# Two slots' shift of a fused projection, with an older head, in an attention and feed-forward kernel

## The chip, the cores and the metric

The kernel runs on one core of a Trainium2 chip. The metric is the time of one execution on the device in microseconds (us). Three executions of the kernel before took 512.79, 513.41 and 513.46 us; the median is 513.41. A core has a matrix engine (PE, with its weight loads shown as PEld), a vector engine (DVE), an activation engine (ACT), a general engine (POOL) and an engine that only issues transfers (SP). They run their own instruction streams in program order and wait for each other through semaphores. The kernel fixes the order of each stream by hand.

## The reference

Attention over 8 batches and 8 heads of 576 rows and 64 columns, with a threshold, and then a feed-forward layer on the joined heads:

```python
scores = scale * np.matmul(q, k.transpose(0, 1, 3, 2))
thresh = np.max(scores, axis=-1, keepdims=True) - tau
scores = np.where(scores >= thresh, scores, -1000000000.0)
attn = np.exp(scores - max) ; attn = attn / (sum(attn) + 1e-09)
x = matmul(attn, v)             # 4608 tokens x 512, heads joined
h = x @ w_in                    # 512 x 2048
g = h * np.clip(h + 3.0, 0.0, 6.0) / 6.0
out = g @ w_out                 # 2048 x 512
```

All inputs and the output are float32.

## The kernel before

**Slots.** Two heads make a pair, two pairs a quad; there are 16 quads. A quad is worked in 9 slots: slots 0 to 3 are the four row tiles of 128 rows of its first pair, 4 to 7 those of the second, and slot 8 the remaining 64 rows of both. So there are 144 slots, numbered n = 0 to 143 in the loop from L539 on, and each holds 128 rows of two heads.

**One slot of attention.** `scores` (L283) multiplies Q by K on PE into PSUM: 576 columns for each of the two heads a, in two parts. `sm_max` (L302) copies a head's scores to SBUF on DVE and takes their row maximum (L310). `sm_bias` (L316) makes the threshold from the maximum on POOL (L317). `sm_mask` (L320) is a rectifier with a huge slope on ACT that rejects what is under the threshold (L322), `sm_exp` (L325) the exponential with its row sum on ACT (L327). `sm_recip` (L329) is a reciprocal on DVE (L330), `sm_norm` (L332) the normalisation to bfloat16 on POOL (L335). The result has to be transposed: by a DMA transpose that SP issues (L343), or, for slots marked `on_chip`, by nine transposes on PE (`pe_transpose`, L346) and a copy on DVE (L351). `av_main` and `av_rest` (L364, L372) multiply the transposed weights by V on PE (L359, L362), and DVE copies the product out as xT or xR (L370, L380). `products` (L507) lists in which slot each product stands.

**Score columns.** Up to slot N1 + 2 each head has one set of PSUM columns for its scores (128 onward for a = 1, 1664 onward for a = 0), so the scores of a slot wait for the maximum of the slot before. Later, odd slots use a second set, 704 and 2240 (`first`, `score_col`, L275 to L281). Slots 1 and 2 have columns of their own (L279), in which the head a = 0 does not wait for that of the slot before, and for these two slots `scores` finishes one head before it begins the other.

**The feed-forward layer.** A first projection item (`mm1`, L385) is 8 matmuls (L394) for two of the sixteen hidden blocks and 256 tokens, or 4 larger ones (L389) for the remaining rows of two batches. Its rectifier (`mm1_relu`, L399) is on ACT in even slots (L402) and on DVE in odd ones (L404); the gate (`mm1_gate`) is on DVE (L417). A finished group of items adds pieces of the second projection (`mm2_part`, L424) to a list: a piece is 4 matmuls (L428), and four pieces make a tile of the output, which is scaled, copied (L434, L436) and written by a DMA. Items are taken one a slot from slot N1 = 22 on (L586), pieces two in each even slot (`second`, L528). Items are put on the list by the products of a quad of odd number (L522 to L525). What the loop leaves over is worked off behind it (L694 to L710).

**Regimes.** From N1 on the order on ACT and DVE changes. Before, in slot n, ACT does the exponentials of slot n - 1 and then the masks of n; from N1 on the exponentials of n and then the masks of n + 1. In even slots from N1 to N2 = 28 DVE takes the maxima of two slots at once (L559, L573), and ACT's exponentials stand ahead of its rectifier (L578).

**Banks.** PSUM has 8 banks of 512 columns. HB = 6 takes the projection items, the PE transposes of on-chip slots and the warm-ups; OB = 7 accumulates the output, and takes the odd slots' items where no pieces were made in the slot before (L590). `bank()` (L216) hands out banks 2 and 5 in turn for transposes of Q and K and for products.

**Head.** `load_quad` (L83) loads Q and K of a quad by DMAs: `load_k`, `load_q`, `rest`. For quad 0 the first K and the rest of K are issued by ACT, everything else by SP. PE starts on two multiplications of a zero constant (L188 to L190) and 14 transposes of the identity (`warm_up`, L191), then it transposes K (L236), the first Q rows (L470), the rest of K (L471) and the other Q rows (L473). Weights of the layer are cast and loaded by DMAs that POOL issues (L165, L169), one or two a slot (L653 to L656).

Of the kernel before, what the change touches and what calls it, by code (L numbers as in the profile page):

```python
# [20 lines left out]
def kernel(  # L21
# [10 lines left out]
    nc = tc.nc  # L32
# [7 lines left out]
    NSLOT = 9  # L40
    NB = 2
    N0 = 3
    N1 = 22
    N2 = 28
    HB, OB = 6, 7
    scale = 1.0 / math.sqrt(D)
    tau = float(tau)
# [35 lines left out]
    def load_quad(quad):  # L83
        b, g = divmod(quad, 2)
        nat[quad] = (nat_pool.tile([P, 1152], F32, tag="nq", name="nq"),
                     nat_pool.tile([P, 4, 4, D], F32, tag="km", name="km"),
                     nat_pool.tile([P, 2 * D], F32, tag="kr", name="kr"))
        nq, km, kr = nat[quad]

        def main(dst, src, h, order, by=nc.sync):  # L90
            by.dma_start(out=dst[:, :, h, :], in_=src[b, 4 * g + h, 0:512, :].rearrange(order, t=4))

        def blocks_q(n, a, j):
            c = 32 * (2 * a + j)
            nc.sync.dma_start(out=nq[c:c + 32, n * S:(n + 1) * S].rearrange("p (k d) -> p k d", d=32),
                              in_=q[b, 4 * g + 2 * n + a, :, 32 * j:32 * j + 32].rearrange("(k r) d -> r k d", r=32))

        def blocks_k(n, a, j):
            c = 32 * (2 * a + j)
            nc.sync.dma_start(  # L100
                out=km[c:c + 32].rearrange("p t h d -> p (t h d)")[:, n * 512:(n + 1) * 512].rearrange(
                    "p (t m d) -> p t m d", t=4, d=32),
                in_=k[b, 4 * g + 2 * n + a, 0:512, 32 * j:32 * j + 32].rearrange("(m r t) d -> r t m d", r=32, t=4))

        def load_k(n):
            if b < NB:
                for a in range(2):
                    main(km, k, 2 * n + a, "(p t) d -> p t d", by=nc.scalar if quad == n == 0 else nc.sync)
            else:
                for a in range(2):  # L110
                    for j in range(2):
                        blocks_k(n, a, j)

        def load_q(n):
            if b < NB:
                for a in range(2):
                    main(nq[:, 0:1024].rearrange("p (t h d) -> p t h d", h=4, t=4), q, 2 * n + a, "(t p) d -> p t d")
            else:
                for a in range(2):
                    for j in range(2):  # L120
                        blocks_q(n, a, j)

        def rest():
            for dst, src in ((kr[:], k), (nq[:, 1024:1152], q))[0:2 if b < NB else 1]:
                for n in range(2):
                    by = nc.scalar if quad == 0 and src is k else nc.sync if quad < 5 else nc.gpsimd
                    by.dma_start(out=dst[64 * n:64 * n + 64, :].rearrange("p (h d) -> p h d", h=2),
                                 in_=src[b, 4 * g + 2 * n:4 * g + 2 * n + 2, 512:S, :].rearrange("h p d -> p h d"))
# [56 lines left out]
        for _ in range(count):  # L185
            nc.tensor.transpose(ps[:, HB, 0:P], identf[:], identf[:])

    blank = nc.const_aps.tensor(0.0, [P, P], F32)  # L188
    for _ in range(2):
        nc.tensor.matmul(ps[:, HB, 0:P], blank, blank, start=True, stop=True)  # L190
    warm_up(14)  # L191
    identb = singles.tile([P, P], BF16)
    nc.vector.tensor_copy(out=identb[:], in_=identf[:])
    three = singles.tile([P, 1], F32)
# [25 lines left out]


    def copy_out(out, in_):
        if 0 <= now < N1 + 2:
            nc.vector.tensor_copy(out=out, in_=in_)
        else:
            nc.scalar.copy(out=out, in_=in_)
# [49 lines left out]
        return n > N1 + 2 and n % 2 == 1  # L276

    def score_col(n, a):
        if n in (1, 2):  # L279
            return 1664 if a else 3200 if n == 1 else 128  # L280
        return (704 if first(n) else 128) + (0 if a else 1536)  # L281

    def scores(n):  # L283
        quad, slot = divmod(n, NSLOT)
        w0 = 320 if first(n) else 384
        parts = ((0, w0), (w0, S - w0))
        heads = range(2)
        for group in [((a,), parts) for a in heads] if n in (1, 2) else [(heads, (part,)) for part in parts]:
            for i in range(2 if slot == 8 else 1):
                for a, (k0, w) in [(a, part) for part in group[1] for a in group[0]]:  # L290
                    pair = 2 * quad + (i if slot == 8 else slot // 4)
                    rows = slice(64 * i, 64 * i + 64) if slot == 8 else slice(0, P)
                    q0 = 512 if slot == 8 else slot % 4 * P
                    c0, kc = score_col(n, a) + k0, 64 * (1 - a) + k0
                    nc.tensor.matmul(ps_flat[rows, c0:c0 + w],  # L295
                                     qT_of(pair)[a * 64:(a + 1) * 64, q0:q0 + rows.stop - rows.start],
                                     kT_of(pair)[a * 64:(a + 1) * 64, kc:kc + w], start=True, stop=True)
# [4 lines left out]
    def sm_max(sl):  # L302
        sl.s = s_pool.tile([P, 2, S], F32, tag="s", name="s")
        sl.m = stat_pool.tile([P, 2], F32, tag="m", name="m")
        sl.bias = stat_pool.tile([P, 2], F32, tag="bias", name="bias")
        sl.rsum = stat_pool.tile([P, 2], F32, tag="rsum", name="rsum")
        sl.rinv = stat_pool.tile([P, 2], F32, tag="rinv", name="rinv")
        for i in range(2):
            c0 = score_col(sl.n, i)
            nc.vector.tensor_scalar(out=sl.s[:, i, :], in0=ps_flat[:, c0:c0 + S],  # L310
                                    scalar1=1.0, scalar2=None, op0=Alu.mult, op1=Alu.max,
                                    accum_out=sl.m[:, i:i + 1])
            if sl.n < N0:
                sm_bias(sl, slice(i, i + 1))

    def sm_bias(sl, of=slice(0, 2)):  # L316
        nc.gpsimd.tensor_scalar(out=sl.bias[:, of], in0=sl.m[:, of], scalar1=-scale, scalar2=tau, op0=Alu.mult,  # L317
                                op1=Alu.add)

    def sm_mask(sl, i):  # L320
        s = sl.s[:, i, :]
# [142 lines left out]

    alloc_qk(0)
    evict = transpose_k(0)
    lead = ps[:, HB:HB + 2, :]
    q_main = nat[0][0][:, 0:1024].rearrange("p (t h d) -> p t h d", h=4, t=4)
    q_rows = bank()
# [14 lines left out]
    for quad in range(NQUAD):  # L484
        for slot in range(NSLOT):
            sl = Slot()
            sl.quad, sl.slot, sl.n = quad, slot, len(queue)
            sl.on_chip = len(queue) < N1 - 1 and (slot in (1, 3, 5, 7, 8) or slot == 0 and quad > 0)
            queue.append(sl)
    scores(0)  # L490
    sm_max(queue[0])
    scores(1)

    turns = {1: [("q", 1), ("k", 1)], 3: [("rest", 0)]}
# [13 lines left out]
    for quad in range(NQUAD):  # L508
        p0, p1 = 2 * quad, 2 * quad + 1
        if quad < NB:  # L510
            jobs = ((8, p0, 0, 512), (13 - 2 * quad, p1, 0, 512), (15 - 3 * quad, None, 0, 0))
        else:
            jobs = [(7 - quad % 2 + 2 * i, *of) for i, of in enumerate(
                ((p0, 0, 256), (p0, 256, 256), (p1, 0, 256), (p1, 256, 256), (None, 0, 0)))]
        for after, *of in jobs:
            products.setdefault(quad * NSLOT + after, []).append((quad, *of))
# [10 lines left out]

    def second():  # L528
        nonlocal pieces, bb, mt, part
        pieces = 2 if now % 2 == 0 and todo2 else 0  # L530
        for _ in range(pieces):
            bb, mt, part = todo2.pop(0)
            mm2_part(bb, mt, part)
# [5 lines left out]
    for n, sl in enumerate(queue):  # L539
# [18 lines left out]
        if n + 1 < len(queue):  # L558
            if n <= N1 or n > N2 + 1 or n % 2 == 0:  # L559
                sm_max(queue[n + 1])  # L560
            if n + 1 >= N0:
                sm_bias(queue[n + 1])
        even = n >= N1 and n % 2 == 0
        if n >= N0:
            sm_recip(prev)
# [20 lines left out]
        if todo1 and n >= N1:  # L586
            item, then = todo1.pop(0)
            if n == len(queue) - 2:
                second()
            h = mm1(item, 0 if n == len(queue) - 1 else OB if n > N1 and n % 2 and not pieces else HB)  # L590
            todo2.extend(then)
        else:
            item = None
# [42 lines left out]
            evict = []  # L636
        for out_of_psum in evict:
            out_of_psum()
        if n < N0:
            scores(n + 2)  # L640
            warm_up(6)
# [11 lines left out]
        if n < 4 or 15 < n < 20 or n > 33:  # L653
            start(vcasts, 1 if n < N1 or n % 2 else 0)
        else:
            start(casts, 2 if n in (5, 8, 11, 14) or 21 < n < 28 else 1)  # L656
        prev = sl

    last = NQUAD - 1
# [85 lines left out]
```

## Time and profile before

| | us |
|---|---|
| three executions | 512.79, 513.41, 513.46 |
| median | 513.41 |
| the profiled execution | 512.79 |
| its span, first to last instruction | 511.0 |
| busy: PE, DVE, ACT, POOL | 503.4, 442.8, 450.3, 298.6 |
| one maximum on DVE (L310), mean | 0.748 |
| one mask, one exponential on ACT (L322, L327), mean | 0.762, 0.671 |
| one normalisation on POOL (L335), mean | 0.743 |
| one gate on DVE (L417), one rectifier on ACT (L402), mean | 0.687, 0.686 |
| one matmul of an item (L394), of a piece (L428), mean | 0.273, 0.379 |

Durations in the groups run from an instruction's start to its end. Neighbours on an engine overlap at their edges, so the distance from one start to the next is shorter: 0.60 for a gate of 0.69, and for a row of 8 item matmuls 0.98 in all. The chain of waits gives such distances. A line of the chain or the timeline has the start in us, the duration or stretch, the engine, the line of the kernel and how many instructions are taken together; in brackets stand the idle time before it and what ended it. In the stretches the number in front of (x..) is an engine's busy time.

### The profile page before, as it was taken

To read this page: it belongs to the slowest core of one execution; us is meant where nothing else is said; L and a number is where in the kernel's file an instruction comes from. 1 tells how busy PE (TensorE), PEld (TensorE's weight loads), DVE (VectorE), ACT (ScalarE), POOL (GpSimd) and SP (SyncE) were. 2 spreads that over 40 slices of the span, in tenths; PEclk is the share of its full clock that TensorE was granted. 3 is DMA by queue.
4 is the path that set the end of the run, shared out by engine and by line. 5 is a ranking of instruction groups with operands and counts; after the bars stand their busy time and mean duration, and the time that the engine had idled before them with its cause. 6 is when DMAs were issued, how large, how long until landed. Compare 5 with 4: busy or idle time off the path is not lost.

```text
span 511.0 us, 12107 instructions
## 1 busy us (share of the span) xinstructions
PE 503.4 (99%) x4132; PEld 319.8 (63%) x4132; DVE 442.8 (87%) x1127; ACT 450.3 (88%) x977; POOL 298.6 (58%) x539
## 2 busy tenths in 40 slices
PE   8999999999999999999999999999999999999997
PEld 7656566666655666666655666666655666667564
DVE  4788899989999999999999999999999999887251
ACT  4999999999999999999999999999999999987160
POOL 2788879666666756656565656666566755552000
PEclk9999999999999999999999999999999999999999
DMA  6998999989999999999899999999999996563132
GB/s 144 182 172 147 153 143 182 174 157 178 188 160 172 163 174 160 205 162 181 150 158 181 154 163 163 179 169 175 163 178 149 187 177 116 114 111 75 72 57 77
DMA packets 314318, 78.77 MB, mean 154 GB/s; under 512 B 296880, under 2 KB 309424, under 8 KB 314256
## 3 DMA queue, kind: packets, MB, share of 16 engines
q1 hardware_dynamic: 294464, 67.90, 78.0%
q0 software_dynamic: 18304, 9.64, 15.6%
q8 instruction: 32, 0.52, 0.4%
q10 hardware_dynamic: 1488, 0.46, 0.4%
q14 instruction: 30, 0.25, 0.2%
HBM read 36.70 MB, written 9.44 MB: 90 GB/s over the span
## 4 chain that ended last, share of the span: by engine, by line
PE 80%; DVE 4%; ACT 3%; issue 1%; DVEq 0%
PE ps L295 24%; PE ps L428 23%; PE ps L394 20%; PE ps L359 7%; PE ps L389 3%; DVE s L310 1%; PE ps L362 1%; ACT s L327 1%; ACT s L322 1%; DVE g L417 1%; DVE r L404 1%; PE ps L668 1%; ACT r L402 1%; PE ps L350 0%; DVE xT L370 0%
## 5 line engine op out<-in xcount | busy, mean ns | idle before, releaser
L335 POOL TENSOR_SCALAR pn<-s,rinv 128x576 bf16<-128x576 f32 x288 | 210.6, 743 | 19.4 <-issue 4.8
L310 DVE TENSOR_SCALAR_CACHE_REDUCE s<-ps 128x576 f32<-128x576 f32 x288 | 205.0, 748 | 13.4 <-POOL pn L335 5.1
L322 ACT ACTIVATE s<-s,bias 128x576 f32<-128x576 f32 x288 | 205.7, 762 | 3.6 <-POOL bias L317 3.2
L327 ACT ACTIVATE s<-s 128x576 f32<-128x576 f32 x288 | 192.5, 671 | 0.3
L295 PE MATMUL ps<-kT,qT 64*128 64x384 f32 (+7 forms) x1280 | 175.5, 419 | 2.1 <-DVE s L310 2.0
L295 PEld LDWEIGHTS ps<-kT,qT 64*128 64x128 f32 (+1 forms) x1280 | 103.7, 175 | 57.8 <-issue 15.6
L394 PE MATMUL ps<-xT,w_in_sb 128*128 128x256 bf16 x1024 | 131.0, 273 | 0.6 <-DVE g L417 0.5
L428 PE MATMUL ps<-w_out_sb,g 128*128 128x512 bf16 x560 | 130.7, 379 | 0.0
L394 PEld LDWEIGHTS <-w_in_sb 128*128 128x128 bf16 x1024 | 95.6, 98 | 40.3 <-issue 21.0
L317 POOL TENSOR_SCALAR bias<-m 128x2 f32<-128x2 f32 (+1 forms) x147 | 27.5, 187 | 148.4 <-DVE rinv L330 132.1
L417 DVE SCALAR_TENSOR_TENSOR g<-r,ps 128x512 bf16<-128x512 f32 x128 | 87.8, 687 | 13.6 <-ACT r L402 9.1
L428 PEld LDWEIGHTS <-g 128*128 128x128 bf16 x560 | 54.6, 98 | 55.0 <-issue 0.4
L402 ACT ACTIVATE r<-ps,three 128x512 f32<-128x512 f32 x81 | 55.4, 686 | 25.1 <-PE ps L394 20.2
L327 ACT ACTIVATION_READ_ACCUMULATOR s<-s 128x1 f32 x288 | 54.5, 189 | 0.0
L404 DVE TENSOR_SCALAR r<-ps 128x512 f32<-128x512 f32 x63 | 42.9, 681 | 0.0
L359 PE MATMUL ps<-pT,vm 128*64 128x256 bf16 (+1 forms) x480 | 39.1, 285 | 0.0
L359 PEld LDWEIGHTS <-vm 128*64 128x64 bf16 x736 | 27.2, 110 | 16.1 <-issue 14.7
L370 DVE CAST xT<-ps 128x256 bf16<-128x256 f32 (+1 forms) x60 | 26.2, 437 | 10.2 <-PE ps L362 10.2
L436 DVE TENSOR_SCALAR osb<-ps 128x512 f32<-128x512 f32 x31 | 20.8, 672 | 8.4 <-PE ps L428 8.4
L310 DVE DVE_READ_ACCUMULATOR s<-ps 128x1 f32 x288 | 23.9, 83 | 0.0
L330 DVE RECIPROCAL rinv<-rsum 128x2 f32<-128x2 f32 x144 | 23.0, 160 | 0.7 <-ACT s L327 0.6
L144 POOL DMA_DIRECT2D vm<-in_v_dram x28 | 21.4, 766 | 0.1
(60 smaller groups left out, 256.6 us busy)
## 6 DMA issues: line engine op xcount, KB each, us to landing
out_dram<-osb SPq DMA_DIRECT2D x31, 256.0 KB, 2.6
nq<-in_q_dram SPq DMA_DIRECT2D x96, 72.0 KB, 3.4
km<-in_k_dram SPq DMA_DIRECT2D x96, 64.0 KB, 3.2
vm<-in_v_dram POOLq DMA_DIRECT2D x24, 128.0 KB, 3.9
nq<-in_q_dram SPq DMA_DIRECT2D x16, 128.0 KB, 4.9
w_in_sb<-in_moe_w_in_dram POOLq DMA_DIRECT2D x16, 128.0 KB, 3.7
w_out_sb<-in_moe_w_out_dram POOLq DMA_DIRECT2D x16, 128.0 KB, 4.1
pT<-pn SPq DMA_TRANSPOSE x117, 3.8
```

The source lines that it names most:

```text
L295: nc.tensor.matmul(ps_flat[rows, c0:c0 + w], qT_of(pair)[a * 64:(a + 1) * 64, q0:q0 + rows.stop - rows.start], kT_of(pair)[a * 64:(a + 1) ...
L310: nc.vector.tensor_scalar(out=sl.s[:, i, :], in0=ps_flat[:, c0:c0 + S], scalar1=1.0, scalar2=None, op0=Alu.mult, op1=Alu.max, accum_out=sl ...
L317: nc.gpsimd.tensor_scalar(out=sl.bias[:, of], in0=sl.m[:, of], scalar1=-scale, scalar2=tau, op0=Alu.mult, op1=Alu.add)
L322: nc.scalar.activation(out=s, in_=s, func=Act.Prelu, bias=sl.bias[:, i:i + 1], scale=scale, alpha=REJECT)
L327: nc.scalar.activation(out=s, in_=s, func=Act.Exp, accum_out=sl.rsum[:, i:i + 1])
L335: nc.gpsimd.tensor_scalar(out=pn[:, i, :], in0=sl.s[:, i, :], scalar1=sl.rinv[:, i:i + 1], scalar2=1.0, op0=Alu.mult, op1=Alu.mult)
L359: nc.tensor.matmul(pb[a * 64:(a + 1) * 64, :], vm[:, 2 * hp + a, c * D:(c + 1) * D], pT[:, 5 * a + c, cols], start=(c == 0), stop=False)
L394: nc.tensor.matmul(ps[:, hb, n * 256:(n + 1) * 256], w_in_sb[:, ki, (ni + n) * P:(ni + n + 1) * P], xT[b][:, ki, c0:c0 + 256], start=(ki = ...
L402: nc.scalar.activation(out=r, in_=hps, func=Act.Relu, bias=three[:])
L404: nc.vector.tensor_scalar(out=r, in0=hps, scalar1=3.0, scalar2=0.0, op0=Alu.add, op1=Alu.max)
L417: nc.vector.scalar_tensor_tensor(out=out, in0=r, scalar=6.0, in1=hps, op0=Alu.min, op1=Alu.mult)
L428: nc.tensor.matmul(o_ps[0], gbuf[:, ni, mt * P:(mt + 1) * P], w_out_sb[:, ni, :], start=(ni == 0), stop=(ni == NI - 1))
```

## The change

The diff puts several edits of the loop in, and takes the special treatment of the first slots out. The loop: N1 goes from 22 to 20 and N2 from 28 to 26, and the thresholds that were written relative to N1 are adjusted, so that the copies of K stay on DVE up to slot 23; slots are transposed on PE only below 17 instead of below 21; the products of quad 1 are put in four jobs, with the second pair in two halves at slots 18 and 21 and the remaining rows at 23, instead of 20 and 21; `second` makes three pieces in slot 36 and one each in 38, 42 and 44; an item in an odd slot after a slot with one piece goes to bank 2 or 5; the weights come two pieces a slot from slot 20 to 26 instead of 22 to 27. The head: K of quad 0 is issued by SP and its first Q by ACT, the rest of K by SP; the zero multiplications go, 14 warm-ups become 17, four more stand behind the transposes of K and eight more in slot 0; slots 1 and 2 use the common score columns and order; the bias of the first three slots is made for both heads at once.

```diff
-    N1 = 22
-    N2 = 28
+    N1 = 20
+    N2 = 26
...
         def load_k(n):
-                    main(km, k, 2 * n + a, "(p t) d -> p t d", by=nc.scalar if quad == n == 0 else nc.sync)
+                    main(km, k, 2 * n + a, "(p t) d -> p t d")
...
         def load_q(n):
-                    main(nq[:, 0:1024].rearrange("p (t h d) -> p t h d", h=4, t=4), q, 2 * n + a, "(t p) d -> p t d")
+                    main(nq[:, 0:1024].rearrange("p (t h d) -> p t h d", h=4, t=4), q, 2 * n + a, "(t p) d -> p t d",
+                         by=nc.scalar if quad == n == 0 else nc.sync)
...
         def rest():
-                    by = nc.scalar if quad == 0 and src is k else nc.sync if quad < 5 else nc.gpsimd
-                    by.dma_start(out=dst[64 * n:64 * n + 64, :].rearrange("p (h d) -> p h d", h=2),
+                    (nc.sync if quad < 5 else nc.gpsimd).dma_start(out=dst[64 * n:64 * n + 64, :].rearrange("p (h d) -> p h d", h=2),
...
-    blank = nc.const_aps.tensor(0.0, [P, P], F32)
-    for _ in range(2):
-        nc.tensor.matmul(ps[:, HB, 0:P], blank, blank, start=True, stop=True)
-    warm_up(14)
+    warm_up(17)
...
     def copy_out(out, in_):
-        if 0 <= now < N1 + 2:
+        if 0 <= now < N1 + 4:
...
     def score_col(n, a):
-        if n in (1, 2):
-            return 1664 if a else 3200 if n == 1 else 128
         return (704 if first(n) else 128) + (0 if a else 1536)
...
-        for group in [((a,), parts) for a in heads] if n in (1, 2) else [(heads, (part,)) for part in parts]:
+        for k0, w in ((0, w0), (w0, S - w0)):
             for i in range(2 if slot == 8 else 1):
-                for a, (k0, w) in [(a, part) for part in group[1] for a in group[0]]:
+                for a in range(2):
...
-            if sl.n < N0:
-                sm_bias(sl, slice(i, i + 1))
...
     evict = transpose_k(0)
+    warm_up(4)
...
-            sl.on_chip = len(queue) < N1 - 1 and (slot in (1, 3, 5, 7, 8) or slot == 0 and quad > 0)
+            sl.on_chip = len(queue) < N1 - 3 and (slot in (1, 3, 5, 7, 8) or slot == 0 and quad > 0)
...
     sm_max(queue[0])
+    sm_bias(queue[0])
...
-            jobs = ((8, p0, 0, 512), (13 - 2 * quad, p1, 0, 512), (15 - 3 * quad, None, 0, 0))
+            jobs = (((8, p0, 0, 512), (9, p1, 0, 256), (12, p1, 256, 256), (14, None, 0, 0)) if quad else
+                    ((8, p0, 0, 512), (13, p1, 0, 512), (15, None, 0, 0)))
...
     def second():
-        pieces = 2 if now % 2 == 0 and todo2 else 0
+        pieces = min(len(todo2), {36: 3, 38: 1, 42: 1, 44: 1}.get(now, 2)) if now % 2 == 0 else 0
...
-            if n + 1 >= N0:
-                sm_bias(queue[n + 1])
+            sm_bias(queue[n + 1])
...
-            h = mm1(item, 0 if n == len(queue) - 1 else OB if n > N1 and n % 2 and not pieces else HB)
+            h = mm1(item, 0 if n == len(queue) - 1 else HB if n <= N1 or n % 2 == 0 or pieces > 1 else
+                    (2, 5)[turn % 2] if pieces else OB)
...
+        if n == 0:
+            warm_up(8)
         if n < N0:
             scores(n + 2)
...
-            start(casts, 2 if n in (5, 8, 11, 14) or 21 < n < 28 else 1)
+            start(casts, 2 if n in (5, 8, 11, 14) or N1 <= n < N1 + 7 else 1)
```

More of the change, by code (lines that the diff above doesn't have):

```diff
@@ L125, in rest @@
                 for n in range(2):
-                    by = nc.scalar if quad == 0 and src is k else nc.sync if quad < 5 else nc.gpsimd
-                    by.dma_start(out=dst[64 * n:64 * n + 64, :].rearrange("p (h d) -> p h d", h=2),
-                                 in_=src[b, 4 * g + 2 * n:4 * g + 2 * n + 2, 512:S, :].rearrange("h p d -> p h d"))
+                    (nc.sync if quad < 5 else nc.gpsimd).dma_start(out=dst[64 * n:64 * n + 64, :].rearrange("p (h d) -> p h d", h=2),
+                                      in_=src[b, 4 * g + 2 * n:4 * g + 2 * n + 2, 512:S, :].rearrange("h p d -> p h d"))
         def both():
@@ L285, in scores @@
         w0 = 320 if first(n) else 384
-        parts = ((0, w0), (w0, S - w0))
-        heads = range(2)
-        for group in [((a,), parts) for a in heads] if n in (1, 2) else [(heads, (part,)) for part in parts]:
+        for k0, w in ((0, w0), (w0, S - w0)):
             for i in range(2 if slot == 8 else 1):
-                for a, (k0, w) in [(a, part) for part in group[1] for a in group[0]]:
+                for a in range(2):
                     pair = 2 * quad + (i if slot == 8 else slot // 4)
@@ L312, in sm_max, with sm_bias @@
                                     accum_out=sl.m[:, i:i + 1])
-            if sl.n < N0:
-                sm_bias(sl, slice(i, i + 1))
-    def sm_bias(sl, of=slice(0, 2)):
-        nc.gpsimd.tensor_scalar(out=sl.bias[:, of], in0=sl.m[:, of], scalar1=-scale, scalar2=tau, op0=Alu.mult,
-                                op1=Alu.add)
+    def sm_bias(sl):
+        nc.gpsimd.tensor_scalar(out=sl.bias[:], in0=sl.m[:], scalar1=-scale, scalar2=tau, op0=Alu.mult, op1=Alu.add)
     def sm_mask(sl, i):
```

## The prediction

> **What bounds the kernel now.** I read the page first, then the busy time by stretch, then the chain of waits, then the timeline of the first 24 us. The page:
>
> ```profile
> span 511.0 us, 12107 instructions
> PE 503.4 (99%) x4132; PEld 319.8 (63%) x4132; DVE 442.8 (87%) x1127; ACT 450.3 (88%) x977; POOL 298.6 (58%) x539
> ```
>
> PE at 99% is an average that hides two regimes: a waiting matmul behind a pipelined one still counts as busy. The stretches separate them (columns: stretch, its length, busy PE, PEld, DVE, ACT, POOL, granted clock, DMA share, GB/s):
>
> ```profile
> 65.60:90.30 24.70, 24.23 (x230) 16.75 (x232) 24.00 (x64) 23.62 (x51) 20.45 (x38) 1.00 1.17 164
> 90.30:109.60 19.30, 18.61 (x167) 11.79 (x164) 18.31 (x48) 18.45 (x42) 12.34 (x23) 1.00 1.09 159
> 109.60:148.20 38.60, 38.60 (x317) 24.36 (x316) 36.15 (x93) 36.73 (x82) 24.98 (x44) 1.00 1.02 172
> ```
>
> Counting reciprocals (one a slot) places slots 20 to 27 in the first, 28 to 33 in the second, 34 to 45 in the third. In the first two DVE and ACT are as full as PE; in the third PE alone has no gap and ACT leaves 1.9 us. The chain says the same (start, us, what):
>
> ```profile
> 77.51 1.44 DVE s L310 x4
> ...
> 97.76 1.33 ACT s L322 x2
> ...
> 112.36 2.14 PE ps L295 x16
> 114.50 0.98 PE ps L394 x8
> 115.48 1.73 PE ps L428 x8
> 117.21 0.87 PE ps L394 x8
> 118.08 0.56 PE ps L359 x8
> 118.64 0.11 PE ps L362 x2
> 118.75 2.14 PE ps L295 x16
> ```
>
> It runs on DVE and ACT until 103.8 and on PE from there to the end. One pair of slots on PE is 2.14 + 0.98 + 1.73 + 0.87 + 0.56 + 0.11 = 6.39 us. ACT needs less: the groups of 109.6 to 148.2 show 2.6 us of idle time before 7 rectifiers (L402), 0.37 a pair, so its pair is 6.0 us with a rectifier; without one (0.57 in the chain), 5.4. Before slot 22 ACT sets the pace: from its first mask at 9.26 to 66 us, the waits of L322 total 2.8 us, of which 2.5 is the very first. So whatever delays that first mask delays everything behind it. The head:
>
> ```profile
> 0.78 1.20 PE L190 MATMUL ps<-const-float32-0.0 128*128 128x128 f32 x4 [0.78 <-PEq L726]
> 1.77 3.19 PE L186 MATMUL ps<-identf 128*128 128x128 f32 x14
> 5.32 0.63 PE L236 MATMUL ps<-identf,km 128*128 128x128 f32 x4 [0.36 <-DMA km<-in_k_dram]
> 8.18 0.76 DVE L310 TENSOR_SCALAR_CACHE_REDUCE s<-ps 128x576 f32<-128x576 f32 x1 [0.53 <-PE ps L295]
> 9.26 1.44 ACT L322 ACTIVATE s<-s,bias 128x576 f32<-128x576 f32 x2 [2.53 <-POOL bias L317]
> 9.71 0.19 POOL L317 TENSOR_SCALAR bias<-m 128x1 f32<-128x1 f32 x1 [0.48 <-DVE s L310]
> ```
>
> The first mask follows the maximum of the first head alone; the second head's bias comes only at 9.71.
>
> **Head, part by part.** (1) One bias for both heads: the first mask then waits for 9.71 + 0.19 + 0.03 = 9.93 instead of 9.26, +0.67. (2) Scores of slots 1 and 2 go back to the shared columns, taken by part instead of by head. Slot 1 then waits for both maxima of slot 0 (read out at 9.62). From the same pattern at slot 4 (maximum ends 16.65, next starts 17.77) the loop takes 1.1 us, so its maximum moves from 9.54 to 10.7. Its bias would be ready about 12.5, its mask is due at 9.93 + 2.68 (four ACT operations) = 12.6: just hidden. The DVE and PE loop is then about 1.0 late where ACT is 0.67 late; at the next slot heavy in DVE copies ACT can meet that difference, so 0.67 to 1.0. (3) Loads: K moves from the ACT queue to SP, the first Q to ACT, the rest of K to SP behind K. Each issue is 0.46 to 0.78 on SP and 0.65 to 0.67 on ACT; K is issued by 1.75 instead of 2.09, Q by 2.09 instead of 1.75, the rest of K by about 3.2, which now stand ahead of the rest of Q (first used in slot 8). ACT issues two DMAs fewer, so its table load starts at 2.1, not 3.5; that was covered. (4) Warm-up: without the zero matmuls PE starts when the identity is there, at 1.4 instead of 0.78. Seventeen transposes at the 0.213 us spacing of the first fourteen end at about 5.0, K is there by then, so its transposes start about 0.3 earlier; the four new warm-ups before Q give most of that back (0.44 at the warm spacing of 0.11). I take -0.1, between -0.3 and +0.4. Eight more warm-ups in slot 0 (0.9 us) stand where PE waits for the maximum of slot 1: nothing, at most 0.9 without that wait. Head: 0.67 to 1.0 less 0.1, I take **+0.7**.
>
> At this place a page has a rule. The first fourteen transposes are spaced 0.213 and those from 5.32 on 0.11: PE got its full rate 4 to 4.5 us after its first matmul, while the profile's clock row prints 1.00 even for 0 to 5 us. The Trainium skill, "TensorE: Matmul & The Clock Gate", section "What's actually happening", says that the clock doubles after a busy window of about 3.4 us and that the windows run freely. By it a start 0.6 later would mostly end in the same window and sometimes a whole window later, which leaves the total at -0.4 in most executions and puts about 2 on it in the others. The sum above goes by the observed spacing alone.
>
> **Middle, part by part.** (5) The projection starts at slot 20 instead of 22. The items of batch 0 are sixteen, one a slot: they end at 35 instead of 37; the next ones are appended by the products of slot 37 in both, so 36 and 37 have none and from 38 on each slot has the item it had. Sixteen pieces of the second projection go to 28, 30, 32, 34 (two each), then 3, 1, 2, 1, 1 at 36 to 44; before, two each at 30 to 44. From 46 on nothing differs, so all is decided between 20 and 46.
>
> Slots 20 to 27 take two items more. DVE: two gates (0.60) and one rectifier (0.61), +1.8; the on-chip slots end at 16 instead of 19, three copies of 0.66 less, -2.0: even. ACT: one rectifier, +0.57, and it waits for the matmuls of slot 20 as it waited for those of slot 22 (0.55). By the timeline the matmuls can start at 66.8 and ACT is free at 67.5: 0.35 lost there, 0.6 at slot 22, against 0.55 before, and some of today's bias waits (0.27, 0.17, 0.10) go. I take **+0.7**; from 0 (hidden) to +1.8 (DVE's relief useless because copies stood in its waits).
>
> Slots 28 to 45, PE against ACT. Pair 28/29 gets two pieces: from ACT's 6.0 to PE's 6.39, +0.4. 30 to 35 as before, 0. Pair 36/37 loses two items (0.98 + 0.87) and gains one piece (0.87): 6.39 - 0.98 = 5.41, ACT without a rectifier 5.4: -1.0. Pairs 38/39, 42/43 and 44/45 lose a piece: PE 5.53, so ACT's 6.0 is the bound: -0.4 each. 40/41: 0. Sum 0.4 - 1.0 - 1.2 = **-1.8**. If ACT and DVE followed PE entirely, three pieces fewer from 38 on are -2.6; if the lighter pairs gain nothing because of DVE (its row: 36.15 busy of 38.60), -0.6.
>
> (6) What goes with it. Three DMA transposes more (slots 17 to 19) on SP: 1.3 us of issue each. SP issues without a pause from 58.0 to 72.5, so slot 20's, issued at 72.7, slips to about 76.7 and lands (3.8 median) at 80.5; its reader, the product of slot 27, is at 85.5: covered by 5 us. Loads behind them slip as far; the next query transposes on DVE are at 88.3. The normalised tile that slot 24 reuses is free at 80.5, needed at 82.2: covered by 1.7, and if not, POOL waits, then DVE. PE loses 27 transposes (0.6 a slot) in its slack. Weights two a slot from 20: POOL spends 0.56 on each issue, its first stretch is 20.45 of 24.70, and slots 20 and 21 add 1.1 in place of as much at 27 and 28 less: 0, at most 1.1. The product of quad 1 in halves: 0.33 + 0.33 against 0.68, 0. The items of 39, 43 and 45 in bank 2 or 5 instead of 6: they avoid the gate of the slot before; 0, or 0.6 (one gate) if a score matmul then waits for that bank. One more bank turn swaps 2 and 5 in all later products: their copies stand ahead of the gate, so 0.
>
> **Sum.** 0.7 + 0.7 - 1.8 = -0.4 us. The profiled execution took 512.79 (span 511.0 and 1.8 around it): 512.4 by its own time. The runs shown are 512.79, 513.41 and 513.46; the median is 0.6 above the profiled one, so 513.0 against 513.41.
>
> **Rivals.** *Full return, 511.4.* ACT's idle 0.37 a pair shows that PE alone binds from slot 34; if ACT and DVE have depth enough, the middle is 0.7 - 2.6 and the first stretch costs only 0.4: -2.2 there, head at its low end, +0.5, less 0.3 of today's waits: -2.0. For it: ACT is idle in the third stretch in every pair. Against: it has only two score buffers a head. *Nothing returned, 513.9.* The burst costs 1.2 because DVE and ACT are both over 95% busy there, and the light pairs return only 36/37 and half the rest: middle -0.4, head +0.9: +0.5. *Slower, 515.0: PE stays at half rate through the first scores.* Place: the stretch up to 9 us. Price: four K transposes, four warm-ups and the five of Q and the rest of K at 0.213 instead of 0.109 (13 x 0.104 = 1.4) and about 0.6 on the first scores, 2.0 on top of -0.4: +1.6. It decides if the full rate comes later than about 6 us; now it has come by 5.3, 4.5 after PE's start, and the same delay from 1.4 gives 5.9. *The shift does not happen* (items waiting for operands at slot 20): the needed products are in slots 17 and 18 and their copies a slot later, so I give it no weight of its own.
>
> **Numbers.** Forecast 0.48, full return 0.22, nothing returned 0.15, half rate 0.15. This kernel's measurement tells about 0.2% (1.0 us) from no change. Forecast: 0.07 faster, 0.36 same, 0.05 slower. Full return: 0.2 faster, 0.02 same. Nothing returned: 0.1 same, 0.05 slower. Half rate: 0.03 same, 0.12 slower. Faster 0.27, same 0.51, slower 0.22. The range 511.3 to 515.0 reaches from the full return to the half rate; the forecast alone is 512.2 to 513.8.
>
> **What would show it.** First mask near 9.9; rows 0.11 apart by 5.3; slot 1's maximum near 10.7. The first rectifier of ACT near 67.9 plus the head's delay; pair 36/37 near 5.4; ACT without gaps from 38 to 45. Wrong if the reciprocal of slot 28 is over 1.5 us later than now, if the chain enters PE before slot 28, or if POOL waits for a DMA transpose between 76 and 84.

## The result and the profile after

The changed kernel took 519.51 us (median of 3 executions, 519.31 to 520.68) against 513.41: 1.0129 times, 95% interval 1.0103 to 1.0155. It is slower by 6 us, outside the range on record (511.3 to 515.0). The profiled execution took 519.51, its span is 517.7. In the file after, lines moved: scores L288, maximum L303, bias L308, mask L312, exponential L317, normalisation L325, DMA transpose L333, products L349 and L352, items L384 and L379, rectifiers L392 (ACT) and L394 (DVE), gate L407, pieces L418. The page:

```profile
span 517.7 us, 12082 instructions
PE 505.2 (98%) x4126; PEld 320.6 (62%) x4126; DVE 441.5 (85%) x1125; ACT 450.8 (87%) x977; POOL 298.1 (58%) x536
```

Hardly any engine works more; the span grew by waits. The three stretches, cut again at the reciprocals of slots 20, 27, 34 and 46 (columns as in the prediction):

```profile
66.80:94.80 28.00, 24.89 (x221) 16.94 (x220) 24.05 (x66) 23.78 (x51) 20.65 (x39) 1.00 1.21 176
94.80:115.00 20.20, 19.63 (x180) 12.46 (x179) 18.52 (x48) 19.05 (x43) 12.16 (x22) 1.00 1.00 152
115.00:153.20 38.20, 37.12 (x291) 23.54 (x290) 34.44 (x90) 35.70 (x80) 24.99 (x44) 1.00 1.10 165
```

They last 28.0, 20.2 and 38.2 us instead of 24.7, 19.3 and 38.6. In the first, DVE and ACT are as busy as before (24.05 against 24.00, 23.78 against 23.62), so the 3.3 us are idle. In the third PE now has 1.1 us of gaps, where it had none. Slot by slot, I subtract the start of each slot's reciprocal (one a slot, DVE; slot n's is the one that stands in slot n of the loop) in the trace before from that after, and call it the lag:

| | lag at its end, us | change | forecast |
|---|---|---|---|
| head, to slot 20 | 1.18 | +1.18 | +0.7 |
| slots 20 to 26 | 2.64 | +1.46 | +0.7 (20 to 27) |
| slots 26 to 27 | 4.45 | +1.81 | 0 |
| slots 27 to 36 | 5.77 | +1.32 | +0.4 |
| slots 36 to 38 | 4.37 | -1.40 | -1.0 |
| slots 38 to 47 | 5.47 | +1.10 | -1.2 |
| slots 47 to 144 | 5.54 | +0.07 | 0 |
| from there to the end of the span | 6.72 | +1.18 | 0 |
| sum | | +6.72 | -0.4 |

The chain of waits from 58 to 160 us (start, us, what) has the places of the second, third and sixth rows:

```profile
72.49 0.61 DVE kT L221
73.15 0.75 PE ps L288 x4
73.97 1.44 DVE s L303 x4
...
80.61 6.77 DMA pT<-pn
...
87.56 1.46 POOL pn L325 x2
...
90.16 0.19 POOL bias L308
90.38 1.44 ACT s L312 x2
...
130.92 0.70 DVE g L407
131.66 0.70 PE ps L288 x2
```

(a) At 73.15 the scores of slot 23 wait for a copy of K (that of pair 6, counted from 0, made in slot 21 through bank 2 or 5, where the second score columns lie). (b) From 80.61 to 87.44 everything hangs on one DMA transpose, that of slot 20: POOL can't overwrite the normalised tile until it has been read, POOL's next bias is late, and so ACT's next mask. (c) At 131.66, and once more at 151.34, the scores of an odd slot wait for the gate of an item in bank 2 or 5.

The waits of 60 to 110 us (who waited for whom: us in all, times, longest) show (b) in two rows of the changed kernel. Before, POOL waited for no transpose there, and ACT's row is that of the second block:

```profile
POOL pn L325 <- DMA pT<-pn: 3.1, 1, 3.1
ACT s L312 <- POOL bias L308: 2.9, 3, 2.5
```

```profile
ACT s L322 <- POOL bias L317: 0.7, 3, 0.3
```

### The profile page after: what moved, and what is told of

Its sections match the earlier page's. It is cut to its first block, busy times and chain, and to the rows that moved or that the text cites. A ratio compares the mean times of both kernels' runs of the same rounds, so it can differ in the third digit from the quotient of the medians.

```text
span 517.7 us, 12082 instructions
## 1 busy us (share of the span) xinstructions
PE 505.2 (98%) x4126; PEld 320.6 (62%) x4126; DVE 441.5 (85%) x1125; ACT 450.8 (87%) x977; POOL 298.1 (58%) x536
## 4 chain that ended last, share of the span: by engine, by line
PE 79%; DVE 5%; DMA 2%; ACT 2%; POOL 0%; issue 0%; POOLq 0%; DVEq 0%
PE ps L288 25%; PE ps L418 23%; PE ps L384 19%; PE ps L349 7%; PE ps L379 2%; DVE g L407 1%; PE ps L352 1%; DMA pT<-pn 1%; DVE s L303 1%; DMA g<-go 1%; DVE r L394 1%; PE ps L663 1%; ACT r L392 1%; ACT s L312 1%; ACT s L317 0%
## 5 line engine op out<-in xcount | busy, mean ns | idle before, releaser
L325 POOL TENSOR_SCALAR pn<-s,rinv 128x576 bf16<-128x576 f32 x288 | 210.7, 743 | 21.5 <-issue 4.5
L303 DVE TENSOR_SCALAR_CACHE_REDUCE s<-ps 128x576 f32<-128x576 f32 x288 | 205.1, 749 | 19.6 <-PE ps L288 8.4
L312 ACT ACTIVATE s<-s,bias 128x576 f32<-128x576 f32 x288 | 205.8, 762 | 7.0 <-POOL bias L308 6.5
L317 ACT ACTIVATE s<-s 128x576 f32<-128x576 f32 x288 | 192.5, 671 | 0.3
L288 PE MATMUL ps<-kT,qT 64*128 64x192 f32 (+7 forms) x1280 | 177.4, 419 | 3.4 <-DVE s L303 1.9
L288 PEld LDWEIGHTS ps<-kT,qT 64*128 64x128 f32 (+1 forms) x1280 | 104.7, 175 | 59.4 <-issue 15.6
L384 PE MATMUL ps<-xT,w_in_sb 128*128 128x256 bf16 x1024 | 131.1, 273 | 0.9 <-DVE g L407 0.8
L418 PE MATMUL ps<-w_out_sb,g 128*128 128x512 bf16 x560 | 131.0, 379 | 0.0
L384 PEld LDWEIGHTS <-w_in_sb 128*128 128x128 bf16 x1024 | 95.6, 98 | 40.7 <-issue 21.3
L308 POOL TENSOR_SCALAR bias<-m 128x2 f32<-128x2 f32 x144 | 26.9, 187 | 152.0 <-DVE rinv L320 136.7
L407 DVE SCALAR_TENSOR_TENSOR g<-r,ps 128x512 bf16<-128x512 f32 x128 | 87.7, 687 | 14.4 <-ACT r L392 10.5
L418 PEld LDWEIGHTS <-g 128*128 128x128 bf16 x560 | 54.5, 98 | 55.3 <-issue 0.7
L392 ACT ACTIVATE r<-ps,three 128x512 f32<-128x512 f32 x81 | 55.3, 686 | 27.3 <-PE ps L384 21.3
L317 ACT ACTIVATION_READ_ACCUMULATOR s<-s 128x1 f32 x288 | 54.5, 189 | 0.0
L394 DVE TENSOR_SCALAR r<-ps 128x512 f32<-128x512 f32 x63 | 42.9, 681 | 0.0
L349 PE MATMUL ps<-pT,vm 128*64 128x256 bf16 (+1 forms) x488 | 39.3, 283 | 0.8 <-DMA pT<-pn 0.8
L349 PEld LDWEIGHTS <-vm 128*64 128x64 bf16 x744 | 27.6, 110 | 17.3 <-issue 15.1
L303 DVE DVE_READ_ACCUMULATOR s<-ps 128x1 f32 x288 | 23.9, 83 | 0.0
```

Of the source, the lines that this page charges most:

```text
L288: nc.tensor.matmul(ps_flat[rows, c0:c0 + w], qT_of(pair)[a * 64:(a + 1) * 64, q0:q0 + rows.stop - rows.start], kT_of(pair)[a * 64:(a + 1) ...
L308: nc.gpsimd.tensor_scalar(out=sl.bias[:], in0=sl.m[:], scalar1=-scale, scalar2=tau, op0=Alu.mult, op1=Alu.add)
L312: nc.scalar.activation(out=s, in_=s, func=Act.Prelu, bias=sl.bias[:, i:i + 1], scale=scale, alpha=REJECT)
L317: nc.scalar.activation(out=s, in_=s, func=Act.Exp, accum_out=sl.rsum[:, i:i + 1])
L325: nc.gpsimd.tensor_scalar(out=pn[:, i, :], in0=sl.s[:, i, :], scalar1=sl.rinv[:, i:i + 1], scalar2=1.0, op0=Alu.mult, op1=Alu.mult)
L349: nc.tensor.matmul(pb[a * 64:(a + 1) * 64, :], vm[:, 2 * hp + a, c * D:(c + 1) * D], pT[:, 5 * a + c, cols], start=(c == 0), stop=False)
```

## The experiments

"Lag" is again against the trace before, and that of each kernel's one profiled execution, which need not be the median one. Each interval is the ratio to the kernel before, run on the same chip.

**The loop without the head.** The head edits undone, the loop as changed: `load_k`, `load_q`, `rest`, warm-ups, `score_col`, `scores` and `sm_bias` as before.

> The changed kernel with the head of the kernel before (its loads, its zero multiplications and 14 warm-ups, its columns and biases of slots 1 and 2); the loop is the changed one. Theory (three separate losses: head, late DMA transposes, items in bank 2 or 5): the reciprocal of slot 20 is back where it stands before the change, 1.2 us earlier than with the change, and all behind it moves by the same, so 1.2 us under the changed kernel, about 518.3. Rival (the head is hidden again by the waits of the loop, because the transposes that slot 24 waits for come at a time that SP sets): less than 0.4 us, 519.1 or more.

517.61 us (515.56 to 518.43), 1.0083 (1.0067 to 1.0098). From slot 20 on the lag grows as in the changed kernel: 0.45 at slot 20, 4.67 at 47. So the loop is the larger part.

**The odd items out of banks 2 and 5.**

```diff
-  h = mm1(item, ... HB if n <= N1 or n % 2 == 0 or pieces > 1 else (2, 5)[turn % 2] if pieces else OB)
+  h = mm1(item, ... HB if n <= N1 or n % 2 == 0 or pieces else OB)
```

> The changed kernel, with the odd items behind one piece back in bank 6. Theory: the scores of the odd slot no longer wait for the gate of the item in bank 2 or 5 (waits of 0.54 us at 131.7 and 151.3 with a gap of 0.97 between score matmuls each); the item itself now waits for the gate of the slot before, about 0.4 us, so 0.3 to 1.0 us less, about 518.8. Rival (slots 38 to 45 are long because DVE is full, whatever the bank): no difference, 519.5, with the wait at another place.

519.36 us (518.11 to 522.67), 1.0135 (1.0111 to 1.0159): by time nothing can be told, as the executions lie 4.6 us apart. By slots of the profiled one (518.11) it can: from 38 to 47 the lag goes from 3.89 to 4.06, +0.17 against +1.10. The scores of the odd slot go without a gap:

```profile
126.78 0.70 DVE g L407
...
127.53 1.03 PE ps L384 x8
...
129.23 2.14 PE ps L288 x16
```

So (c) costs about 0.9 us. But the lighter slots return nothing here either: in bank 6 the item at 127.53 waits for the gate at 126.78, that of the item before it.

**Two pieces again in 36 to 42.**

```diff
-  pieces = min(len(todo2), {36: 3, 38: 1, 42: 1, 44: 1}.get(now, 2)) if now % 2 == 0 else 0
+  pieces = min(len(todo2), 2) if now % 2 == 0 else 0
```

> The changed kernel with two pieces in each even slot again (36, 38, 40, 42 two each, 44 none), so no item goes to bank 2 or 5. Theory: pair 36/37 stays near 5.2, 38/39 to 42/43 go back to the 6.4 of before, 44/45 falls to ACT's 6.0, so slots 38 to 46 take about 0.8 us less than with the change: 518.7. Rival (the light pairs are as good as they can be): 0.5 us more than the changed kernel, 520.0.

517.87 us (517.54 to 519.33), 1.0102 (1.0087 to 1.0116). From slot 36 to 47 the lag falls by 1.49, from 5.08 to 3.59; in the changed kernel it falls by 0.30. The spread over 36 to 44 is worse than two a slot, by 1.2 us. But 0.95 of this is the bank wait of (c), which this run does not have either: with the light pairs kept and the items in bank 6 (the run before this one), the lag falls by 1.25 from 36 to 47. Only about 0.25 is left for the spread itself.

**Slots 17 to 19 on PE again, in the changed kernel.**

```diff
-  sl.on_chip = len(queue) < N1 - 3 and ...
+  sl.on_chip = len(queue) < N1 + 1 and ...
```

> The changed kernel with slots 17, 18 and 19 transposed on PE again. Theory (three DMA transposes too many on SP make slot 20's late by 6.8 us, POOL waits 3.1 for it and ACT 2.5): POOL's wait for a DMA transpose and ACT's wait of 2.5 at slot 25 go, minus up to 1 us for the copies on DVE in slots 20 to 22: 1.5 to 2.5 us less, about 517.5. Rival (the burst is limited by DVE and ACT, and the wait only stands where another would stand): 0 to 1 us more, 519.5 to 520.5.

524.79 us (522.36 to 526.15), 1.0224 (1.0205 to 1.0242). A miss: 6.3 us are lost between the reciprocals of slots 21 and 22, because the PE transposes share bank 6 with the items: in its chain a gate at 70.87 releases nine PE transposes at 71.61, their copy on DVE at 72.31 releases the next item at 73.12, and so on. PE works in order, so all behind it waits too. The jump from 26 to 27 is gone (11.16 at both), but so much else moved that this run can't stand for it.

**SP's last loads of quad 4 spread.** For quad 4 alone: its remaining rows stay in slot 20, the K of its second pair (k1) goes to 22 and 23, two DMAs each.

```diff
-  loads.extend((lambda: load_q(0), lambda: load_k(0), lambda: load_q(1), both))
+  loads.extend((lambda: load_q(0), lambda: load_k(0), lambda: load_q(1), rest, lambda: k1(0), lambda: k1(1)))
```

> The changed kernel; quad 4's last loads, six DMAs of 4 us of issue in slot 20 on SP, are spread: the rest of K in slot 20, K of its second pair two DMAs each in slots 22 and 23. Theory (slot 20's DMA transpose is late because it stands behind these loads on SP): it is issued near 78 instead of 80.6 and lands near 83 instead of 87.4, POOL waits for it no more, ACT's wait of 2.5 at slot 25 goes, and rows 26 to 27, where the lag against the kernel before grows by 1.8, show under 0.4: about 1.5 to 2.5 us less, 517.5. Rival (the transposes are slow by themselves, as the DMA engines are full): the lag still grows by over 1 us there, 519 or more.

518.05 us (517.66 to 519.24), 1.0101 (1.0084 to 1.0118). Between slots 26 and 27 nothing is lost now (2.85 at both), and from 26 to 30 0.77 instead of 2.86. POOL still waits 1.7 us for a transpose, ACT's longest wait for a bias falls from 2.5 to 0.3. With the spread, slot 20's transpose was issued at 77.31 and landed at 82.64, instead of 80.61 and 87.38. So it was SP's order. SP's rows show it, of the kernel before and of the changed one (start, duration to the last issue of the row, what):

```profile
67.21 1.32 SPq L127 DMA_DIRECT2D kr<-in_k_dram  x2
68.58 3.94 SPq L100 DMA_DIRECT2D km<-in_k_dram  x4
72.69 15.23 SPq L343 DMA_TRANSPOSE pT<-pn  x6
```

```profile
73.03 3.37 SPq L333 DMA_TRANSPOSE pT<-pn  x1
76.45 1.36 SPq L127 DMA_DIRECT2D kr<-in_k_dram  x2
77.85 2.66 SPq L100 DMA_DIRECT2D km<-in_k_dram  x4
80.61 10.33 SPq L333 DMA_TRANSPOSE pT<-pn  x5
```

In both the six last loads of quad 4 stand ahead of slot 20's transpose (L343, L333, the first of its row). In the changed kernel they stand behind a transpose whose issue took 3.37.

**A fifth normalised tile.**

```diff
-  pn_pool = ... name="pn", bufs=4
+  pn_pool = ... name="pn", bufs=5
-  o_pool = ... name="op", bufs=3
+  o_pool = ... name="op", bufs=2
```

> The changed kernel with five buffers of the normalised tile instead of four, and two output buffers instead of three to make room. Theory: POOL's normalisation of slot 24 no longer waits for slot 20's transpose; the transpose itself is as late as before, so PE still waits up to 1 us for it in slot 27 (0.8 now): the growth of 1.8 at rows 26 to 27 falls to 0.5 to 1.0, 518.5. Rival (POOL's wait is not on the path): growth of 1.8 as with four.

518.04 us (517.67 to 519.55), 1.0099 (1.0082 to 1.0115). Again no jump at 27 (3.13 at both). Slot 20's transpose was as late as in the changed kernel (it landed at 86.99), so here it hurts through the reuse of its source, not through its reader: PE's expected wait at the product did not come. A new one of 0.5 us, for a weight DMA at 101.5, did.

**K of pair 6 transposed in slot 20.**

```diff
-  first_odd + (0, 2, 3, 5, 7)[i]
+  first_odd + (0, 1, 3, 5, 7)[i]
```

> The changed kernel with the transposes of the keys of pair 6 in slot 20 instead of 21. Theory (they lie in bank 2 or 5 until DVE has copied them, and the first scores in the second set of columns, those of slot 23, need these banks): the score matmul at 73.1 no longer waits for the copy of K, DVE's gap of 0.88 before the maximum of slot 23 falls under 0.3, and the lag at rows 23 to 26 is 0.5 to 0.8 less. The total may hide it, as SP's transposes are as late as before: 0 to 0.8 us less. Rival (the gap is the length of PE's own work in slots 20 and 21): the gap stays and the lag is the same.

519.18 us (518.59 to 520.16), 1.0117 (1.0102 to 1.0132). From slot 20 to 23 the lag grows by 0.41 instead of 0.98, so (a) costs 0.6. At 27 the late transpose takes it back (+2.16).

**All of it: head of before, spread loads, K in slot 20, two pieces.**

> The loop of the changed kernel with the head of before, the loads spread, the keys in slot 20 and two pieces a slot (e1, e3, e5 and e7 together). Theory: head 0 to 0.4, slots 20 to 28 under +1.0, slots 28 to 46 about -1.0 to -1.5: between 512.3 and 513.8, near the kernel before. Rival (the burst at slot 20 loses by DVE and ACT being full, and what I name are places and not causes): over 515.

514.90 us (513.87 to 516.04), 1.0033 (1.0023 to 1.0043): 1.1 above the upper end of what the theory gave, and 0.1 under the rival's 515, so this time decides for neither. The lag is 0.31 at slot 20, 1.20 at 26, 2.14 at 30, 0.70 at 38, 0.93 at 47.

**Only the head, on the kernel before.**

> The kernel before with the head of the changed one: loads, warm-ups, columns and biases of the first slots; the loop is that of before. Theory (ACT sets the pace to slot 33, so the head's delay passes through whole): rows 1 to 20 are 1.2 to 2.0 later, as in all kernels with that head, and the end as much: 514.2 to 515.0 against 513.2. Rival (waits behind the head take the delay up): under 0.5 us.

514.39 us (513.88 to 515.75), 1.0029 (1.0019 to 1.0040). The lag is 1.87 at slot 2 and 1.89 at the end: nothing behind it absorbs a late head.

**Only the loads and warm-ups of the head, on the kernel before.**

> The kernel before with only the loads and warm-ups of the changed head; columns and biases of slots 1 and 2 stay as before. Theory (the bias for both heads at once costs 0.67 and the common columns the rest): -0.1 to +0.3 us, 513.0 to 513.5. Rival (the later start of PE and the other order of the loads cost most of the head): +0.6 to +1.0.

513.89 us (513.09 to 516.27), 1.0017 (1.0007 to 1.0027); lag 0.52 at slot 2, 1.08 at the end. This is no gain of 0.1 but a loss of about half a us: the first scores start 0.23 later, and the other 0.29 comes behind them, where eight warm-ups more stand. The half us that the lag grows by behind slot 60 (at slots 94, 95 and 112) was not followed up.

What differs between executions of one head is when PE reaches its full rate. It shows in the distance between equal PE transposes, 0.21 us before and 0.11 after. The PE rows of the changed kernel, and of the one with PE transposes in 17 to 19, which has the same head (start, stretch, what):

```profile
5.14 0.66 PE L233 MATMUL ps<-identf,km 128*128 128x128 f32 x4
5.63 0.60 PE L186 MATMUL ps<-identf 128*128 128x128 f32 x4
...
7.04 1.33 PE L288 MATMUL ps<-kT,qT 64*128 64x384 f32 x8
```

```profile
5.08 1.08 PE L233 MATMUL ps<-identf,km 128*128 128x128 f32 x4
5.96 1.06 PE L186 MATMUL ps<-identf 128*128 128x128 f32 x4
...
7.99 1.33 PE L288 MATMUL ps<-kT,qT 64*128 64x384 f32 x8
```

In the first the four transposes of K take 0.49 from their start to that of the next row; in the second 0.88, the four warm-ups behind them 0.85 (the next row starts at 6.81), and the first scores start 0.95 later. In the eight traces with the whole new head the first scores start between 7.03 and 7.99 (mean 7.46), before at 6.90; the lag at slot 2 less that delay is 1.04 or 1.05 in every one. In the eight with the old loads and warm-ups they start between 6.85 and 7.38 (mean 7.03). So one bias, the common columns and the eight warm-ups in slot 0 cost 1.04 together, and the later warm-up about 0.4 on the mean, 1.1 at most. The Trainium skill, "TensorE: Matmul & The Clock Gate", section "What's actually happening", says that the window is free-running and that the moment of the change varies by half a us either way; here it lay from about 3.5 to 5.9 us after the first matmul, which is wider.

**No pieces in slot 28**, on the mended version (`and now != 28` behind the condition).

> As e8, but no pieces in slot 28: two each in 30 to 44, as in the kernel before. What differs from before is then the two items in slots 20 and 21 instead of 36 and 37 with what belongs to them. Theory (the pieces in slot 28 make PE late there, +0.94 in rows 26 to 30 of e8, and the pieces freed from 44 return as much later): rows 26 to 30 add under 0.5, rows 44 to 47 no longer gain 0.4: between -0.4 and +0.2 against e8, 514.5 to 515.1. Rival (slots 28 to 30 are late because DVE and ACT come late out of the burst): +0.9 at rows 26 to 30 again, and 515.3.

516.14 us (513.40 to 517.39), 1.0050 (1.0029 to 1.0072). From slot 26 to 30 the lag still grows by 0.79 (0.94 in the mended version); a product waits 1.7 us for a DMA transpose. By these two traces the pieces of slot 28 are about 0.15 of what those slots lose. The time scatters too much to tell more: the profiled execution took 514.23, four of the seven 516.1 to 517.4.

**Only slots 17 to 19 by DMA, on the kernel before.**

```diff
-  sl.on_chip = len(queue) < N1 - 1 and ...
+  sl.on_chip = len(queue) < N1 - 5 and ...
-  jobs = ... (15 - 3 * quad, None, 0, 0))
+  jobs = ... (15 - quad, None, 0, 0))
```

> The kernel before with slots 17 to 19 transposed by DMA instead of on PE, and the rest product of quad 1 in slot 23 instead of 21 so that it does not wait; nothing else. Theory (the three DMA transposes delay that of slot 20 on SP, and the normalisation of slot 24 waits for it): POOL waits for a DMA transpose before slot 24's normalisation, and rows 26 to 27 are 0.7 to 2 later; three copies on DVE less give back up to 0.5: 513.7 to 515.0. Rival (only the earlier burst makes that transpose late): no wait on a transpose, 513.2 or less.

The second line moves the product of quad 1's remaining rows from slot 21 to 23. 515.77 us (514.75 to 518.45), 1.0066 (1.0046 to 1.0085). Lag 0 at slot 26, 1.52 at 28, 1.70 at 29 and to the last slot; ACT waits 0.9 and 0.6 for a bias. The transposes of slots 20 and 21 land at 83.41 and 87.22, and 0.18 behind each POOL starts the normalisation that reuses the tile, at 83.59 after 1.5 of idle time and at 87.40 after 1.0. (The list of waits puts these two down to ACT and DVE, whose work was done by then.) The product that reads both starts at 87.35, after 1.8 of idle time of PE. Three DMA transposes more, without any earlier item, cost this.

**The same with the loads spread.**

> e12 (the kernel before with three more DMA transposes) with quad 4's last six loads spread as in e5. Theory A (the loads in front of the transposes on SP make them late): the lag of 1.7 between rows 26 and 29 falls under 0.6, 513.3 to 514.3. Theory B (the DMA engines are full in this stretch and each transpose takes 5 to 7 us whatever stands in front): the lag stays over 1.2, 515 or more.

513.64 us (513.05 to 518.74), 1.0029 (1.0009 to 1.0049). Seven of the twelve executions took 513.05 to 513.82, five 514.80 to 518.74. The profiled one (513.06) is of the first kind: the lag is -0.03 all along from slot 29 to 144, and the waits that are left (us in all, times, longest) cost nothing. What the other five lose was not profiled; late transposes there are not excluded.

```profile
PE ps L365 <- DMA pT<-pn: 1.1, 1, 1.1
...
POOL pn L341 <- DMA pT<-pn: 0.7, 2, 0.4
...
ACT s L328 <- POOL bias L323: 0.4, 2, 0.2
```

**The spread alone, on the kernel before** (a control).

> The kernel before with quad 4's last loads spread, as a control. Both theories: no transpose is waited for in the kernel before, so no difference, 512.9 to 513.5.

512.94 us (512.64 to 513.55), 0.9999 (0.9990 to 1.0007). The spread is worth nothing where no transpose is waited for.

**The mended version with five tiles.**

> e8 (all mended, head of before) with five buffers of the normalised tile and two output buffers. Theory A: nothing waits for a transpose before slot 28 in e8, so no gain there; the wait of 0.26 and 0.11 at slots 26 and 29 goes: 0 to 0.5 under e8, 514.2 to 514.9. Theory B (e8 varies from 513.9 to 516.0 between executions because transposes land late in some): the executions come closer together, and the median falls by 0.5 to 1.0, 513.9 to 514.4.

513.83 us (513.68 to 514.76), 1.0017 (1.0008 to 1.0025), against 514.90 without the fifth tile, and half the scatter (1.1 us against 2.2). This fits late transposes in the mended version. In the profiled execution with four tiles POOL waits 0.3 for slot 22's, and 1.9 for slot 23's: that one lands at 93.87, and the normalisation of slot 27 starts at 94.05 (the list of waits puts this down to DVE). What the scatter itself comes from, no trace of a late execution shows. With five tiles the lag is 0 at slot 20, 0.88 at 26, 1.64 at 30, 0.22 at 38, 0.44 at 47. No version was faster than the kernel before.

## Why the prediction was wrong

**Step (6), three DMA transposes more at nothing: 2.1 us.** This step and the light pairs below (2.3, the bank wait among it) are the two largest misses. The prediction had slot 20's transpose issued at 76.7 and landing after 3.8; it was issued at 80.6 and landed after 6.8, so 87.4 instead of 80.5, and the cover of 1.7 for the reused tile was short by 5 (by 3.1 in the trace, where POOL itself came 2 later). Two mistakes met. An issue was priced at 1.3, the row of a free queue, and slot 17's took 2.6, slot 19's 3.4. And 3.8 was the median of the whole run, while in this stretch even the kernel before had 5.1 (4.5 to 6.4); after, 5.5 (4.5 to 7.5). Price: from slot 26 to 30 the lag grows by 2.86, with the loads spread by 0.77, so 2.1. The prediction had named the wait ("if not, POOL waits, then DVE") and left it at nothing; the sign it gave, POOL waiting for a DMA transpose, came at 84.5 to 87.6, and the reciprocal of slot 28 was 4.46 later, where 1.5 had been the limit.

**Items in bank 2 or 5, "0, or 0.6".** It was about 0.9 together, at two of the slots, as the chain shows at 131.66 and 151.34.

**The light pairs, -1.2.** They returned nothing, rather +0.2 without the bank wait, where two pieces a slot have +0.2 as well. The sum took a pair's PE work against ACT's; but with one piece less PE stands at the item until the gate of the item before frees bank 6. Work that is taken from an engine that waits returns nothing. Pair 36/37 (said -1.0, measured -1.4) was right: there the items themselves are missing, and their bank wait with them.

**The head, +0.7.** One bias, the common columns and the eight warm-ups of slot 0 cost 1.04 together, the upper end of what was worked out for the first two (first mask at 10.07, said 9.9; slot 1's maximum at 10.77, said 10.7). The eight warm-ups were put at nothing; with the old biases and columns 0.29 was lost where they stand, so part of the 1.04 may be theirs. The loads and warm-ups were put at -0.1 and cost 0.1 to 1.1, about half a us. The rival of half rate was right in kind: the full rate came as late as 7.2, and in another execution at 5.2. Its 2.0 was too much, since the first scores themselves were never slow (eight take 1.33 us in both PE views above).

**Slots 20 to 27, +0.7.** To slot 26 it is 1.46; 0.6 of it is the wait for K's copy in bank 2 or 5, which the prediction did not see. With that mended 0.9 is left, near the 0.7, inside the bounds of 0 to 1.8. Whether it is what the prediction summed up is not shown. A rival for it stands: two weights a slot from slot 20, put at 0, at most 1.1. In the last version POOL's normalisations of slots 21 to 26 follow each other 2.9 to 3.1 us apart with hardly a gap (so do those of slots 23 to 27 in the kernel before, at 2.9), and the two weight issues are 1.12 of that; no run moved the weights alone.

**Slots 28 to 30, +0.4.** Where POOL waits for no transpose, in the two versions with five tiles, it is 0.76. The pieces of slot 28 are about 0.15 of it; what the rest is, was not tried apart. The prediction also placed its first stretch wrongly by one slot: by the reciprocals 90.30 begins slot 27, not 28. No term of the sum rests on that.

**The end, 0.** Of 1.18 us, 0.53 is a transpose for the last gates, which PE needs and whose landing took 4.8 (4.1 before). The other 0.65 comes behind the last instruction of DVE, where only stores are left. Why, and why kernels with the same loop end 0.3 to 1.2 later, stays open.

Added up, the early start costs 0.9 in slots 20 to 26 and 0.8 in 26 to 30 even when every named wait is mended (last version), and 30 to 47 gives 1.2 back: the shift is worth a small loss, not the -1.1 that the sum gave it without the head, and the rest of the 6 us are waits that it brought along, the head and the end.

## What to carry to other kernels

When a step is moved to a queue that issues in order, write the queue down slot by slot and take durations from the stretch in which it will run, not from the run's median: a transpose took 3.8 in the median of the run and 6.8 here. Follow a late transfer to the buffer that it reads, not only to its reader. Count work that is taken off an engine as a gain only where the engine works through; where it stops at a bank, lighten what the bank waits for.

## What was not expected of the hardware

The share of the hardware queue in the stretch from 66 to 90 us rose from 59.6% to 76.8% of the 16 engines' time, for 2.65 instead of 2.39 MB, before and after:

```profile
q1 hardware_dynamic: 12126, 2.39, 59.6%
```

```profile
q1 hardware_dynamic: 13834, 2.65, 76.8%
```

So 11% more bytes went with 29% more of the engines' time; eight transposes were issued in this stretch after the change, seven before. Whether the transposes themselves take that time, or packets that wait for one another, no run here shows. The Q loads landed after 4.9 us (median) instead of 3.4, the K loads after 3.8 instead of 3.1; but in the control, the kernel before with the loads spread and no transpose more, the same K loads took 4.8, so this is not the transposes' doing alone. The moment at which PE reaches its full rate moved by 2 us between executions of the same head.
